# A two-layer transformer kernel: the DMA queue of SyncE put into one fixed, written order

## The chip, the cores and the metric

One core of a Trainium2 chip runs the kernel. The metric is the device time of one execution in microseconds (us), as a median over runs. All runs in this document were of the undisturbed ("fast") state. The engines are called PE (TensorE, the matrix engine), PEld (its weight loads), DVE (VectorE), ACT (ScalarE), POOL (GpSimd) and SP (SyncE, which here does nothing but issue DMA transfers). The program fixes an order for the instructions of each engine, and for the transfers that SyncE issues; the timelines below show what that does when a transfer has to wait (at the first place looked at, SyncE issues nothing for 30 us).

## The reference

`x` is 2048 tokens by 1024 channels in bfloat16. Two layers, with the same weights, each add an attention over 8 positions (its own and 7 earlier ones, every second one) and a gated feed-forward part:

```python
x = x + A(layernorm(x))       # q,k,v = x @ wqkv ; 32 heads of 32; window 8, dilation 2 ; o @ wo
x = x + B(layernorm(x))       # (relu(x @ W_gate) * (x @ W_up)) @ W_down,  inner width 3584
x = x + A(layernorm(x))
x = x + B(layernorm(x))
```

## The kernel before

The tokens are cut into 4 blocks of 512. Blocks 0 to 3 are the first layer, 4 to 7 the second, so that `n` runs from 0 to 7. The kernel is software-pipelined. For each `n`, TensorE does gate and up of block `n`, then Q, K (and V) of block `n+2`, then the output projection "wo" of block `n+1`, then the down projection of block `n` in two halves of the output channels. Meanwhile VectorE does the attention arithmetic of later blocks, and the second norm of block `n+1` is worked out during the down projection.

Weights stream through a ring of five slots of 1 MB ("slabs"). A slab may be asked for once TensorE has finished with the slab that used its slot:

```python
wring = ctx.enter_context(tc.tile_pool(name="wring", bufs=5))

def load_slab(src_ap, name):
    t = wring.tile([P, 8, SLAB], BF16, tag="slab", name=name)
    ...
    tail_sp[0] = nc.sync.dma_start(tv, src_ap).ins      # SyncE's queue
    return tv
```

The second norm, cut to what matters. Statistics and the scaled copy are on ScalarE, one power on 128 numbers is on GpSimd, and the transfer that transposes the whole block is issued, in SyncE's queue, right with the last tile:

```python
def apply(t):
    def f():
        nc.scalar.activation(xn, xt[:], ACT.Identity, scale=..., bias=...)     # normalised tile t
        if which == "b" and n == 0:
            nc.sync.dma_start_transpose(hold["xnT"][:, t, :, :], xn)
        elif t == TPB - 1:                                                     # TPB = 4 tiles of 128 tokens
            nc.sync.dma_start_transpose(hold["xnT"][...], hold["xn"][...])
    return f
# in the statistics of each tile:
#   nc.gpsimd.tensor_tensor(rstd, vpe, neg_half[:, 0:1], op=ALU.pow)
```

The down projection asks for its slab inside the step that uses it. There are eight steps, four slabs for each half:

```python
def f_(half, s8):
    def f():
        wsl = load_slab(wd_v[:, 8 * s8:8 * s8 + nfc, half * SLAB:(half + 1) * SLAB], ...)
        for t in range(TPB): ...   # 8 matmuls of 128x512 per tile, 32 per slab (half as many for the last slab of a half)
```

Everything is emitted from a list of `(time, function)` pairs sorted by time. A scheduler then fixes each engine's order, unless `tc.issue_after(ins)` pins an instruction behind another.

## Time and profile before

| | |
|---|---|
| time, median of 4 runs | 1721.78 us (1721.57 to 1723.26) |
| TensorE busy | 1637.0 us, 95% of the span of 1719.2 us |
| idle before the second half of the down projection | 56.2 us in six waits |

From the page of the kernel before, part 1 (busy us, share of the span, instructions), part 2 (40 equal slices of the span; PEclk is the granted TensorE clock in tenths, 9 standing for 90% and more) and part 4 (the chain of work that ended last):

```profile
PE 1637.0 (95%) x7576; PEld 781.2 (45%) x7576; DVE 1047.8 (61%) x888; ACT 534.5 (31%) x1117; POOL 273.7 (16%) x220
PEclk9999999899998999989999899998999989999999
PE 65%; DVE 11%; ACT 5%; POOL 4%; issue 3%; DMA 2%; SPq 2%; DVEq 0%; ACTq 0%; POOLq 0%
```

TensorE is the limit, yet the chain is on TensorE for only 65% of the span; six single slices show a lower clock. The waits of TensorE in the kernel before (engine, tile and line, what it waited for, then total us, times, longest us):

```profile
PE dacc_2642 L104 <- DMA wd_1_0_2646<-in_B_W_down_dram: 12.2, 1, 12.2
PE dacc_3999 L104 <- DMA wd_1_0_4003<-in_B_W_down_dram: 12.2, 1, 12.2
PE tp L226 <- DVE xn_first L208: 9.2, 1, 9.2
PE dacc_9780 L104 <- DMA wd_1_0_9784<-in_B_W_down_dram: 8.1, 1, 8.1
PE dacc_5446 L104 <- DMA wd_1_0_5450<-in_B_W_down_dram: 8.0, 1, 8.0
...
PE acc_g L104 <- DMA xnT_b_1207<-xn_b_1206: 5.1, 1, 5.1
PE acc_wo L104 <- DMA oT_1055<-o_d: 2.4, 1, 2.4
```

All six long waits are for `wd_1_0`, the first slab of the second half of the down projection. To see why it is late, look at SyncE's timeline at the first of them (start us, duration us, queue, line, kind of transfer, out<-in). The duration is how long SyncE took to issue the transfer, not how long it took to land (the slab at 331.87 us: 0.52 us to issue, 5.6 us from there to landing):

```profile
294.23 0.37 SPq L151 DMA_DIRECT2D wd_0_3_2613<-in_B_W_down_dram  x1
294.64 1.86 SPq L399 DMA_DIRECT2D vhm_2567<-v_d  x1
326.87 4.90 SPq L186 DMA_TRANSPOSE xnT_b_2429<-xn_b_2428  x1
331.87 0.52 SPq L151 DMA_DIRECT2D wd_1_0_2646<-in_B_W_down_dram  x1
```

SyncE issues nothing for 30 us, then the transpose, then the slab, whose slot had been free since about 301 us. TensorE's timeline (in brackets: how long it was idle before, and until what) shows the price:

```profile
324.25 1.03 PE L104 MATMUL dacc_2482<-wd_0_3_2613,hT_1392 128*128 128x512 bf16 x4
337.51 3.60 PE L104 MATMUL dacc_2642<-wd_1_0_2646,hT_1392 128*128 128x512 bf16 x8 [12.23 <-DMA wd_1_0_2646<-in_B_W_down_dram]
340.89 2.03 PE L104 MATMUL dacc_2643<-wd_1_0_2646,hT_1392 128*128 128x512 bf16 x8
```

After 12.23 us of nothing the first eight matmuls take 3.60 us where others take 1.89.

### The profile page before, as it was taken

The page shows a single profiled execution, that of the slowest core. Times are in us where ns is not written, and L with a number is a line of the kernel's source. Part 1 is how long each engine was busy: PE and PEld are TensorE (multiplying, and loading weights), DVE is VectorE, ACT ScalarE, POOL GpSimd, SP SyncE. Part 2 cuts the span into 40 slices and gives each one's busy share as a digit, 9 for nine tenths or more (in the row PEclk, how much of TensorE's full clock was granted, in tenths as well). Part 3 has the DMA queues.
Part 4 walks back from the last instruction along what each step waited for, and adds up shares of the span by engine and source line. Part 5 has one row for each costly group of instructions (what it writes and reads, how often), then busy time and mean ns, then how long its engine had stood idle before and what let it go on. Part 6 is the DMA issues. An engine that isn't in the chain of part 4 may idle for free.

```text
span 1719.2 us, 18662 instructions
## 1 busy us (share of the span) xinstructions
PE 1637.0 (95%) x7576; PEld 781.2 (45%) x7576; DVE 1047.8 (61%) x888; ACT 534.5 (31%) x1117; POOL 273.7 (16%) x220
## 2 busy tenths in 40 slices
PE   7998999799997999989999899998999989999999
PEld 3543445344553445434454344543445434444444
DVE  1699698947296854938459384692936929221211
ACT  7936412314231422314224051240513401130110
POOL 1322005301061101101042010520105100000000
PEclk9999999899998999989999899998999989999999
DMA  9476748466556483774846738458484484656442
GB/s 291 80 209 156 200 147 224 103 190 185 182 131 187 150 220 117 185 190 147 221 142 159 212 125 248 148 126 244 135 252 148 110 256 150 196 171 195 148 143 79
DMA packets 370791, 296.82 MB, mean 173 GB/s; under 512 B 142352, under 2 KB 351248, under 8 KB 369680
## 3 DMA queue, kind: packets, MB, share of 16 engines
q1 hardware_dynamic: 370416, 295.10, 60.3%
q8 instruction: 59, 0.97, 0.2%
q10 hardware_dynamic: 288, 0.52, 0.1%
q14 instruction: 28, 0.23, 0.0%
HBM read 256.77 MB, written 21.00 MB: 162 GB/s over the span
## 4 chain that ended last, share of the span: by engine, by line
PE 65%; DVE 11%; ACT 5%; POOL 4%; issue 3%; DMA 2%; SPq 2%; DVEq 0%; ACTq 0%; POOLq 0%
PE acc_g L104 23%; PE acc_u L104 22%; PE acc_q L104 3%; SPq L186 2%; PE acc_k L104 1%; POOL st_b_3784 L173 1%; PE acc_wo L104 1%; DVE ac_0_7810 L363 1%; DVE ac_0_9257 L363 1%; DVE ac_0_6367 L363 1%; POOL st_b_5235 L173 0%; POOL st_b_6679 L173 0%; POOL st_b_8122 L173 0%; PE dacc_5446 L104 0%; PE dacc_6890 L104 0%
## 5 line engine op out<-in xcount | busy, mean ns | idle before, releaser
L482 ACT ACTIVATE r<-acc_g 128x512 bf16<-128x512 f32 x224 | 132.5, 594 | 769.3 <-PE acc_g L104 760.8
L483 DVE TENSOR_TENSOR hT_10981<-acc_u,r 128x512 bf16<-128x512 f32 x28 | 19.4, 692 | 77.4 <-PE acc_u L104 77.4
L483 DVE TENSOR_TENSOR hT_9913<-acc_u,r 128x512 bf16<-128x512 f32 x28 | 19.3, 688 | 38.4 <-PE acc_u L104 38.4
L483 DVE TENSOR_TENSOR hT_8466<-acc_u,r 128x512 bf16<-128x512 f32 x28 | 19.2, 688 | 38.3 <-PE acc_u L104 36.0
L483 DVE TENSOR_TENSOR hT_4132<-acc_u,r 128x512 bf16<-128x512 f32 x28 | 19.2, 688 | 38.3 <-PE acc_u L104 36.0
L483 DVE TENSOR_TENSOR hT_2775<-acc_u,r 128x512 bf16<-128x512 f32 x28 | 19.2, 688 | 38.3 <-PE acc_u L104 36.0
L483 DVE TENSOR_TENSOR hT_7019<-acc_u,r 128x512 bf16<-128x512 f32 x28 | 19.2, 688 | 38.3 <-PE acc_u L104 36.0
L483 DVE TENSOR_TENSOR hT_5575<-acc_u,r 128x512 bf16<-128x512 f32 x28 | 19.2, 688 | 38.0 <-PE acc_u L104 35.7
L104 PEld LDWEIGHTS <-hT_1392 128*128 128x128 bf16 x224 | 22.3, 100 | 40.2 <-DMA wd_1_0_2646<-in_B_W_down_dram 12.7
L104 PEld LDWEIGHTS <-hT_2775 128*128 128x128 bf16 x224 | 22.3, 100 | 40.2 <-DMA wd_1_0_4003<-in_B_W_down_dram 12.7
L104 PEld LDWEIGHTS <-hT_8466 128*128 128x128 bf16 x224 | 22.4, 101 | 36.7 <-DMA wd_1_0_9784<-in_B_W_down_dram 8.6
L104 PEld LDWEIGHTS <-hT_7019 128*128 128x128 bf16 x224 | 22.5, 101 | 36.4 <-DMA wd_1_0_8337<-in_B_W_down_dram 8.3
L104 PEld LDWEIGHTS <-hT_5575 128*128 128x128 bf16 x224 | 22.5, 101 | 36.3 <-DMA wd_1_0_6894<-in_B_W_down_dram 8.3
L104 PEld LDWEIGHTS <-hT_4132 128*128 128x128 bf16 x224 | 22.4, 100 | 36.3 <-DMA wd_1_0_5450<-in_B_W_down_dram 8.5
L104 PEld LDWEIGHTS <-hT_9913 128*128 128x128 bf16 x224 | 21.9, 98 | 26.4
L104 PEld LDWEIGHTS <-hT_10981 128*128 128x128 bf16 x224 | 21.9, 98 | 26.4
L483 DVE TENSOR_TENSOR hT_1392<-acc_u,r 128x512 bf16<-128x512 f32 x28 | 19.2, 686 | 17.1 <-PE acc_u L104 12.6
L173 POOL TENSOR_TENSOR st_b_10661<-st_b_10661,neg_half 128x1 f32<-128x1 f32 x4 | 2.2, 550 | 159.2 <-ACT st_b_10661 L172 159.2
L329 DVE TENSOR_TENSOR prod_426<-q_0_373,k_0_411 128x4096 bf16<-128x4096 bf16 x1 | 2.3, 2293 | 27.7 <-ACT k_0_411 L296 27.7
L173 POOL TENSOR_TENSOR st_a_8704<-st_a_8704,neg_half 128x1 f32<-128x1 f32 x4 | 6.7, 1680 | 73.3 <-ACT st_a_8704 L172 73.3
L173 POOL TENSOR_TENSOR st_a_5814<-st_a_5814,neg_half 128x1 f32<-128x1 f32 x4 | 6.7, 1682 | 73.2 <-ACT st_a_5814 L172 73.2
L173 POOL TENSOR_TENSOR st_a_7257<-st_a_7257,neg_half 128x1 f32<-128x1 f32 x4 | 6.7, 1680 | 73.2 <-ACT st_a_7257 L172 73.2
(1942 smaller groups left out, 4063.1 us busy)
## 6 DMA issues: line engine op xcount, KB each, us to landing
vhm_375<-v_d SPq DMA_DIRECT2D x4, 284.0 KB, 5.4
vhm_1441<-v_d SPq DMA_DIRECT2D x4, 284.0 KB, 10.0
vhm_2567<-v_d SPq DMA_DIRECT2D x4, 284.0 KB, 9.1
vhm_3924<-v_d SPq DMA_DIRECT2D x4, 284.0 KB, 9.5
vhm_5376<-v_d SPq DMA_DIRECT2D x4, 284.0 KB, 5.8
vhm_6820<-v_d SPq DMA_DIRECT2D x4, 284.0 KB, 5.8
vhm_8263<-v_d SPq DMA_DIRECT2D x4, 284.0 KB, 5.8
vhm_9710<-v_d SPq DMA_DIRECT2D x4, 284.0 KB, 6.3
```

Source lines behind the costliest of these rows:

```text
L104: tail_pe[0] = nc.tensor.matmul(*args, **kwargs).ins
L173: nc.gpsimd.tensor_tensor(rstd, vpe, neg_half[:, 0:1], op=ALU.pow)
L186: nc.sync.dma_start_transpose(hold["xnT"][:].rearrange("p t k n -> p (t k) n"), hold["xn"][:].rearrange("p t d -> p (t d)"))
L329: nc.vector.tensor_tensor(prods[c][:], i0, i1, op=ALU.mult)
L363: nc.vector.tensor_tensor(o, ac[:], t[:], op=ALU.add)
L482: nc.scalar.activation(r[:], acc[:], ACT.Relu)
L483: nc.vector.tensor_tensor(hold["hT"][:, j, :], accs["u"][:], r[:], op=ALU.mult)
```

## The change

The intent: SyncE's order is written down in full instead of being left to the scheduler. A weight slab is asked for at the time its ring slot is planned to be free, and every other transfer gets a written place between slabs, where its data are planned to be ready. Each transfer is pinned behind the one before it. The same matmuls are done in the same order. The diff, cut to its core:

```diff
+    def sp_dma(dst, src, transpose=False):
+        start = nc.sync.dma_start_transpose if transpose else nc.sync.dma_start
+        ...
+            with tc.issue_after(tail_sp[0]):
+                tail_sp[0] = start(dst, src).ins
-    def load_slab(src_ap, name): ...
+    def want(key, src, use_end):
+        slab_plan.append((key, src, use_end))          # every slab of the kernel, with the end of its use
+    def slab_events(events):
+        for i, (key, src, _) in enumerate(slab_plan):
+            def f(...): ... sp_dma(tv, src) ...
+            events.append((slab_plan[i - RING][2] + 0.3 if i >= RING else 0.1 * i, f))
         def apply(t):
-                elif t == TPB - 1:
-                    nc.sync.dma_start_transpose(hold["xnT"]..., hold["xn"]...)
+        def turn(t=None):                               # the transpose, now an event of its own
+                    sp_dma(hold["xnT"]..., hold["xn"]..., True)
...
-            ln2(n + 1, [at + GRP * TPB + GRP * (t + 1) + 0.1 for t in range(TPB)])
+            ln2(n + 1, [at + GRP * TPB + GRP * (t + 1) + 0.1 for t in range(TPB)], at + 2 * GRP * TPB + 31.0)
...                                                      # the opening (blocks 0 to 3 before the first gate/up):
-    ln1(3, 85.0, True)
+    ln1(3, 85.0, t_v2 + 2.0, True)                      # transpose of block 3's first norm
+    ev.append((t_v2 + 3.0, store_v(1)))
+    ev.append((t_v2 + 10.0, store_o(0)))                # attention output of block 0: store, then load transposed
+    ev.append((t_v2 + 10.1, load_o(0)))
```

With the `+ 31.0` the transpose stands behind all the slabs of the down projection. Stores and loads of V and of the attention output are made events of their own in the same way.

More of the change, by code (lines that the diff above doesn't have):

```diff
@@ L56 @@
     NSL = (FC + 7) // 8
+    NSG = (FC + 3) // 4
+    RING = 5
     scale = float(DH) ** -0.5
@@ L71 @@
     dram = ctx.enter_context(tc.tile_pool(name="dram", bufs=1, space=bass.MemoryType.DRAM))
-    wring = ctx.enter_context(tc.tile_pool(name="wring", bufs=5))
+    wring = ctx.enter_context(tc.tile_pool(name="wring", bufs=RING))
     xnT_pool = ctx.enter_context(tc.tile_pool(name="xnT", bufs=2))
@@ L93 @@
     tail_sp = [None]
+    def sp_dma(dst, src, transpose=False):
+        start = nc.sync.dma_start_transpose if transpose else nc.sync.dma_start
+        if tail_sp[0] is None:
+            tail_sp[0] = start(dst, src).ins
+        else:
+            with tc.issue_after(tail_sp[0]):
+                tail_sp[0] = start(dst, src).ins
     @contextmanager
@@ L138, with load_x @@
         x_tiles.append(xt)
-    def load_x(b, alternate=False):
+    def load_x(b):
         for t in range(b * TPB, (b + 1) * TPB):
-            eng = nc.scalar if alternate and t % 2 else nc.sync
-            eng.dma_start(x_tiles[t][:], x_dram[t * P:(t + 1) * P, :])
-    load_x(0, alternate=True)
-    def load_slab(src_ap, name):
-        shp = list(src_ap.shape)
-        t = wring.tile([P, 8, SLAB], BF16, tag="slab", name=name)
-        tv = t[:, 0:shp[1], 0:shp[2]]
-        tail_sp[0] = nc.sync.dma_start(tv, src_ap).ins
-        return tv
+            if b == 0 and t % 2:
+                nc.scalar.dma_start(x_tiles[t][:], x_dram[t * P:(t + 1) * P, :])
+            else:
+                sp_dma(x_tiles[t][:], x_dram[t * P:(t + 1) * P, :])
@@ new lines, with want_v, want_qk @@
+    load_x(0)
+    slab = {}
+    slab_plan = []
+    def want(key, src, use_end):
+        slab_plan.append((key, src, use_end))
+    def want_v(key, mid, end):
+        for g in range(2):
+            want((key, g), wqkv_v[:, :, 2 * D + g * SLAB:2 * D + (g + 1) * SLAB], mid if g == 0 else end)
+    def want_qk(key, end):
+        for i, nm in enumerate(("q", "k")):
+            for hh in range(2):
+                want((key, nm, hh), wqkv_v[:, hh * (KC // 2):(hh + 1) * (KC // 2), i * D:(i + 1) * D], end)
@@ new lines, in want_wo, with want_gu, want_down @@
+    def want_wo(n, mid, end):
+        for half in range(2):
+            want(("o", n, half), wo_v[:, :, half * SLAB:(half + 1) * SLAB], mid if half == 0 else end)
+    def want_gu(n, at, gap):
+        for s in range(NSG):
+            cols = slice(s * SLAB, min((s + 1) * SLAB, F))
+            end = at + gap * min(4 * (s + 1), FC)
+            want(("g", n, s), wg_v[:, :, cols], end)
+            want(("u", n, s), wu_v[:, :, cols], end)
+    def want_down(n, at, gap):
+        for half in range(2):
+            for s in range(NSL):
+                rows = slice(8 * s, min(8 * (s + 1), FC))
+                end = at + gap * (half * FC + min(8 * (s + 1), FC))
+                want(("d", n, half, s), wd_v[:, rows, half * SLAB:(half + 1) * SLAB], end)
@@ new lines, in slab_events, with f @@
+    def slab_events(events):
+        for i, (key, src, _) in enumerate(slab_plan):
+            def f(key=key, src=src):
+                shp = list(src.shape)
+                t = wring.tile([P, 8 * SLAB], BF16, tag="slab", name="w_" + "_".join(str(k) for k in key))
+                tv = t[:, 0:shp[1] * shp[2]].rearrange("p (a b) -> p a b", b=shp[2])
+                sp_dma(tv, src)
+                slab[key] = tv
+            events.append((slab_plan[i - RING][2] + 0.3 if i >= RING else 0.1 * i, f))
@@ L179, in f @@
             def f():
-                xt = x_tiles[b * TPB + t]
-                xn = hold["xn"][:, t, :]
-                nc.scalar.activation(xn, xt[:], ACT.Identity, scale=hold["st"][:, t, 4:5], bias=hold["st"][:, t, 6:7])
-                if which == "b" and n == 0:
-                    nc.sync.dma_start_transpose(hold["xnT"][:, t, :, :], xn)
-                elif t == TPB - 1:
-                    nc.sync.dma_start_transpose(hold["xnT"][:].rearrange("p t k n -> p (t k) n"),
-                                                hold["xn"][:].rearrange("p t d -> p (t d)"))
-            return f
-        return [stats(t) for t in range(TPB)], [apply(t) for t in range(TPB)], hold
+                nc.scalar.activation(hold["xn"][:, t, :], x_tiles[b * TPB + t][:], ACT.Identity,
+                                     scale=hold["st"][:, t, 4:5], bias=hold["st"][:, t, 6:7])
+            return f
+        def turn(t=None):
+            def f():
+                if t is not None:
+                    sp_dma(hold["xnT"][:, t, :, :], hold["xn"][:, t, :], True)
+                else:
+                    sp_dma(hold["xnT"][:].rearrange("p t k n -> p (t k) n"),
+                           hold["xn"][:].rearrange("p t d -> p (t d)"), True)
+            return f
+        return [stats(t) for t in range(TPB)], [apply(t) for t in range(TPB)], turn, hold
     def ln_first():
@@ L234, with v_steps @@
     att = [{} for _ in range(NN)]
-    def v_steps(n, ln, sl=None, early=False):
-        b = n % NB
+    def v_steps(n, ln, key, early=False):
         st = att[n]
-        sl = {} if sl is None else sl
         def f_(c):
@@ L243, in f @@
                 g = c // 4
-                if g not in sl:
-                    sl[g] = load_slab(wqkv_v[:, :, 2 * D + g * SLAB:2 * D + (g + 1) * SLAB], f"wv_{n}_{g}")
                 if c == 0:
@@ L251, in f, with store_v @@
                     for kc in range(KC):
-                        mm(acc[:], lhsT=sl[g][:, kc, col:col + P], rhs=ln["xnT"][:, :, kc, :],
-                                         start=(kc == 0), stop=(kc == KC - 1))
+                        mm(acc[:], lhsT=slab[(key, g)][:, kc, col:col + P], rhs=ln["xnT"][:, :, kc, :],
+                           start=(kc == 0), stop=(kc == KC - 1))
                 nc.scalar.copy(st["vT"][:, c, :], acc[:])
-                if c == KC - 1:
-                    dst = bass.AP(tensor=v_d.tensor, offset=v_d.offset + HALO + b * BLK,
-                                  ap=[[NTOK, P], [P * NTOK, KC], [1, BLK]])
-                    nc.sync.dma_start(dst, st["vT"][:])
             return f
         return [f_(c) for c in range(KC)]
+    def store_v(n):
+        def f():
+            dst = bass.AP(tensor=v_d.tensor, offset=v_d.offset + HALO + (n % NB) * BLK,
+                          ap=[[NTOK, P], [P * NTOK, KC], [1, BLK]])
+            sp_dma(dst, att[n]["vT"][:])
+        return f
     khalo = {}
@@ L269, with qk_steps @@
     K_STEP = [QK_ORDER.index(("k", c)) for c in range(KC)]
-    def qk_steps(n, ln, sl=None):
+    def qk_steps(n, ln, key):
         b = n % NB
         st = att[n]
-        sl = {} if sl is None else sl
         def f_(nm, c):
@@ L278, in f @@
                 if nm == "q" and c == 0:
-                    for i, w in enumerate(() if sl else ("q", "k")):
-                        for hh in range(2):
-                            t = wring.tile([P, KC // 2, D], BF16, tag="slab", name=f"w{w}_{n}_{hh}")
-                            tail_sp[0] = nc.sync.dma_start(t[:], wqkv_v[:, hh * (KC // 2):(hh + 1) * (KC // 2), i * D:(i + 1) * D]).ins
-                            sl[(w, hh)] = t
                     khalo[n] = qk_pool.tile([P, KC, HALO], BF16, tag="kh", name=f"kh_{n}", bufs=2)
@@ L287, in f @@
                     for kc in range(KC):
-                        w = sl[(nm, kc // (KC // 2))][:, kc % (KC // 2), bass.ds(c, P, KC)]
+                        w = slab[(key, nm, kc // (KC // 2))][:, kc % (KC // 2), bass.ds(c, P, KC)]
                         mm(acc[:], lhsT=w, rhs=ln["xnT"][:, :, kc, :], start=(kc == 0), stop=(kc == KC - 1))
@@ L397, in f @@
                               ap=[[DH * NTOK, H], [NTOK, DH], [1, HALO + P]])
-                with tc.issue_after(tail_sp[0]):
-                    nc.sync.dma_start(att[n]["v_hm"][32 * tq:32 * tq + 32, :, :], src)
+                sp_dma(att[n]["v_hm"][32 * tq:32 * tq + 32, :, :], src)
             return f
@@ L419, in f, with store_o, load_o @@
                 nc.vector.tensor_tensor(ohm[:, g * DG:(g + 1) * DG, :], tt[:, 0], tt[:, 1], op=ALU.add)
-                if g == NG - 1:
-                    dst = bass.AP(tensor=o_d.tensor, offset=o_d[b * TPB:b * TPB + 1].offset, ap=[[DH * P, P], [1, DH * P]])
-                    nc.sync.dma_start(dst, ohm[:].rearrange("p d t -> p (d t)"))
-                    oTa = big_tile([P, KC, TPB, P], f"oT_{n}")
-                    for tq in range(TPB):
-                        src = bass.AP(tensor=o_d.tensor, offset=o_d[b * TPB + tq:b * TPB + tq + 1].offset,
-                                      ap=[[P, P], [P * P, KC], [1, P]])
-                        nc.sync.dma_start(oTa[:, :, tq, :], src)
-                    st["oT"] = oTa
             return f
         return [f_(g) for g in range(NG)]
+    def store_o(n):
+        def f():
+            b = n % NB
+            dst = bass.AP(tensor=o_d.tensor, offset=o_d[b * TPB:b * TPB + 1].offset, ap=[[DH * P, P], [1, DH * P]])
+            sp_dma(dst, att[n]["o_hm"][:].rearrange("p d t -> p (d t)"))
+        return f
+    def load_o(n):
+        def f():
+            b = n % NB
+            oTa = big_tile([P, KC, TPB, P], f"oT_{n}")
+            for tq in range(TPB):
+                src = bass.AP(tensor=o_d.tensor, offset=o_d[b * TPB + tq:b * TPB + tq + 1].offset,
+                              ap=[[P, P], [P * P, KC], [1, P]])
+                sp_dma(oTa[:, :, tq, :], src)
+            att[n]["oT"] = oTa
+        return f
     def wo_steps(n):
@@ L435, in wo_steps @@
         st = att[n]
-        sl = {}
         order = [(t, half) for t in range(TPB) for half in range(2)]
@@ L444, in f @@
                 for t, half in order[2 * i:2 * i + 2]:
-                    if half not in sl:
-                        sl[half] = load_slab(wo_v[:, :, half * SLAB:(half + 1) * SLAB], f"wo_{n}_{half}")
                     xt = x_tiles[b * TPB + t]
@@ L450, in f @@
                         for c in range(KC):
-                            mm(acc[:], lhsT=st["oT"][:, c, t, :], rhs=sl[half][:, c, :],
-                                             start=(c == 0), stop=(c == KC - 1))
+                            mm(acc[:], lhsT=st["oT"][:, c, t, :], rhs=slab[("o", n, half)][:, c, :],
+                               start=(c == 0), stop=(c == KC - 1))
                     xs = xt[:, half * SLAB:(half + 1) * SLAB]
@@ L467, in f @@
                 s4, jl = j // 4, j % 4
-                if jl == 0:
-                    ncol = min(SLAB, F - s4 * SLAB)
-                    hold["g"] = load_slab(wg_v[:, :, s4 * SLAB:s4 * SLAB + ncol], f"wg_{n}_{s4}")
-                    hold["u"] = load_slab(wu_v[:, :, s4 * SLAB:s4 * SLAB + ncol], f"wu_{n}_{s4}")
                 accs = {}
@@ L476, in f @@
                         for kc in range(KC):
-                            mm(acc[:], lhsT=hold[nm][:, kc, jl * P:(jl + 1) * P], rhs=ln["xnT"][:, :, kc, :],
-                                             start=(kc == 0), stop=(kc == KC - 1))
+                            mm(acc[:], lhsT=slab[(nm, n, s4)][:, kc, jl * P:(jl + 1) * P], rhs=ln["xnT"][:, :, kc, :],
+                               start=(kc == 0), stop=(kc == KC - 1))
                     accs[nm] = acc
@@ L498, in f @@
                 nfc = min(8, FC - 8 * s8)
-                wsl = load_slab(wd_v[:, 8 * s8:8 * s8 + nfc, half * SLAB:(half + 1) * SLAB], f"wd_{n}_{half}_{s8}")
+                wsl = slab[("d", n, half, s8)]
                 for t in range(TPB):
@@ L510, in f, with store_x @@
                         nc.vector.tensor_tensor(xs, ac[t], xs, op=ALU.add)
-                        if n >= NN - NB and half == 1:
-                            nc.sync.dma_start(out_dram[(b * TPB + t) * P:(b * TPB + t + 1) * P, :], xt[:])
             return f
         return [f_(half, s8) for half in range(2) for s8 in range(NSL)]
+    def store_x(n):
+        def f():
+            for t in range((n % NB) * TPB, (n % NB + 1) * TPB):
+                sp_dma(out_dram[t * P:(t + 1) * P, :], x_tiles[t][:])
+        return f
     def emit(events):
@@ L524, with spread @@
     GRP = 1.73
-    def spread(events, steps, at, gap):
+    def spread(steps, at, gap):
         for i, f in enumerate(steps):
-            events.append((at + gap * i, f))
+            ev.append((at + gap * i, f))
     ev = []
@@ L536, in zero_v, with ln1, ln2 @@
     def zero_v():
-        nc.sync.dma_start(bass.AP(tensor=v_d.tensor, offset=v_d.offset, ap=[[NTOK, P], [P * NTOK, KC], [1, HALO]]), zpad[:])
-    def ln1(n, at, early=False, gap=3.0):
-        stats, apply, hold = ln_steps(n, "a", early)
+        sp_dma(bass.AP(tensor=v_d.tensor, offset=v_d.offset, ap=[[NTOK, P], [P * NTOK, KC], [1, HALO]]), zpad[:])
+    def ln1(n, at, turn_at, early=False, gap=3.0):
+        stats, apply, turn, hold = ln_steps(n, "a", early)
         ln_a[n] = hold
-        spread(ev, stats, at, gap)
-        spread(ev, apply, at + 2.0 * gap, gap)
-    def ln2(n, ats):
-        stats, apply, hold = ln_steps(n, "b")
+        spread(stats, at, gap)
+        spread(apply, at + 2.0 * gap, gap)
+        ev.append((turn_at, turn()))
+    def ln2(n, ats, turn_at=None):
+        stats, apply, turn, hold = ln_steps(n, "b")
         ln_b[n] = hold
@@ L550, in ln2 @@
             ev.append((a + 4.0, apply[t]))
-    wqk, wv23 = {}, {}
-    ev.append((12.0, zero_v))
-    ev.append((13.0, lambda: load_x(1)))
-    spread(ev, v_steps(0, ln_a[0], early=True), 15.0, GRP)
-    ln1(1, 20.0, True)
-    at = 29.0
-    gap = 2.1
-    spread(ev, qk_steps(0, ln_a[0], wqk), at, gap)
+            if turn_at is None:
+                ev.append((a + 9.0, turn(t)))
+        if turn_at is not None:
+            ev.append((turn_at, turn()))
+    GAP0 = 2.05
+    t_v0 = 15.0
+    t_qk0 = t_v0 + GRP * KC
@@ new lines @@
+    t_qk1 = t_qk0 + GAP0 * 2 * KC
+    t_v1 = t_qk1 + GRP * 2 * KC + 1.5
+    t_v2 = t_v1 + GRP * KC
+    t_wo0 = t_v2 + GRP * KC
+    t_v3 = t_wo0 + GRP * KC
+    t_gu0 = t_v3 + GRP * KC
+    ev.append((0.45, zero_v))
+    ev.append((0.5, lambda: load_x(1)))
+    want_v("v0", t_v0 + GRP * KC / 2, t_qk0)
+    want_qk("qk01", t_v1)
+    spread(v_steps(0, ln_a[0], "v0", early=True), t_v0, GRP)
+    ln1(1, 22.0, 47.5, True, 5.0)
+    ev.append((t_qk0 + 1.5, store_v(0)))
+    spread(qk_steps(0, ln_a[0], "qk01"), t_qk0, GAP0)
@@ L561 @@
     mults, reds = prod_direct_steps(0)
     for c in range(KC):
-        ev.append((at + gap * (K_STEP[c] + 1.0), mults[c]))
+        ev.append((t_qk0 + GAP0 * (K_STEP[c] + 1.0), mults[c]))
         if c < KC - 2:
-            ev.append((at + gap * (K_STEP[c] + 2.5), reds[c]))
-    spread(ev, load_v_steps(0), 31.0, 7.0)
-    ev.append((45.0, lambda: load_x(2)))
-    at += gap * 2 * KC
-    spread(ev, qk_steps(1, ln_a[1], wqk), at, GRP)
-    ev.append((at + 0.5 * GRP, reds[KC - 2]))
-    ev.append((at + 1.5 * GRP, reds[KC - 1]))
@@ L572 @@
-    ev.append((at + 1.6 * GRP, lambda: softmax(0)))
-    spread(ev, pv_steps(0), at + 10.0, 4.2)
-    ln1(2, 60.0, True)
-    ev.append((70.0, lambda: load_x(3)))
-    sums1, red1 = prod_sum_steps(1)
-    spread(ev, sums1, at + 46.0, 4.4)
-    at += GRP * 2 * KC
-    spread(ev, v_steps(1, ln_a[1], wv23, True), at, GRP)
-    at += GRP * KC
-    ln1(3, 85.0, True)
-    spread(ev, v_steps(2, ln_a[2], wv23, True), at, GRP)
-    at += GRP * KC
-    spread(ev, wo_steps(0), at, 2 * GRP)
-    ln2(0, [at + 2 * GRP * (t + 1) + 0.1 for t in range(TPB)])
@@ L586 @@
-    at += 2 * GRP * TPB
-    spread(ev, v_steps(3, ln_a[3], wv23), at, GRP)
-    at += GRP * KC
-    spread(ev, load_v_steps(1), at + 6.0, 9.0)
-    ev.append((at + 48.1, red1))
-    ev.append((at + 48.2, lambda: softmax(1)))
-    ev.append((at - 0.01, start_hidden))
+            ev.append((t_qk0 + GAP0 * (K_STEP[c] + 2.5), reds[c]))
+    spread(load_v_steps(0), t_qk0 + 5.0, 6.0)
+    ev.append((50.0, lambda: load_x(2)))
+    spread(qk_steps(1, ln_a[1], "qk01"), t_qk1, GRP)
+    ev.append((t_qk1 + 0.5 * GRP, reds[KC - 2]))
@@ new lines @@
+    ev.append((t_qk1 + 1.5 * GRP, reds[KC - 1]))
+    ev.append((t_qk1 + 1.6 * GRP, lambda: softmax(0)))
+    spread(pv_steps(0), t_qk1 + 10.0, 4.2)
+    ln1(2, 60.0, t_qk1 + 15.0, True)
+    ev.append((70.0, lambda: load_x(3)))
+    want_v("v123", t_v3 + GRP * KC / 2, t_gu0)
+    spread(v_steps(1, ln_a[1], "v123", True), t_v1, GRP)
+    ln1(3, 85.0, t_v2 + 2.0, True)
+    ev.append((t_v2 + 3.0, store_v(1)))
+    spread(v_steps(2, ln_a[2], "v123", True), t_v2, GRP)
+    ev.append((t_v2 + 10.0, store_o(0)))
@@ new lines @@
+    ev.append((t_v2 + 10.1, load_o(0)))
+    ev.append((t_wo0 + 3.0, store_v(2)))
+    sums1, red1 = prod_sum_steps(1)
+    spread(sums1, t_qk1 + 46.0, 4.4)
+    want_wo(0, t_v3, t_v3)
+    spread(wo_steps(0), t_wo0, 2 * GRP)
+    ln2(0, [t_wo0 + 2 * GRP * (t + 1) + 0.1 for t in range(TPB)])
+    spread(v_steps(3, ln_a[3], "v123"), t_v3, GRP)
+    ev.append((t_gu0 + 3.0, store_v(3)))
+    spread(load_v_steps(1), t_gu0 + 6.0, 7.0)
+    ev.append((t_gu0 + 48.1, red1))
+    ev.append((t_gu0 + 48.2, lambda: softmax(1)))
@@ L594 @@
+    ev.append((t_gu0 - 0.01, start_hidden))
+    at = t_gu0
     for n in range(NN):
         gu, hold = gu_steps(n, ln_b[n])
-        spread(ev, gu, at, 2 * GRP)
+        want_gu(n, at, 2 * GRP)
+        spread(gu, at, 2 * GRP)
         if n == 0:
-            spread(ev, pv_steps(1), at + 58.0, 5.5)
+            spread(pv_steps(1), at + 58.0, 5.5)
+            ev.append((at + 105.0, store_o(1)))
+            ev.append((at + 105.1, load_o(1)))
         elif n + 1 < NN:
@@ L601 @@
             ev.append((at + 0.2, lambda n=n: softmax(n + 1)))
-            spread(ev, pv_steps(n + 1), at + 12.0, 6.5)
+            spread(pv_steps(n + 1), at + 12.0, 6.5)
+            ev.append((at + 72.0, store_o(n + 1)))
+            ev.append((at + 72.1, load_o(n + 1)))
         if n + 2 < NN:
-            ln1(n + 2, at + 30.0)
+            ln1(n + 2, at + 30.0, at + 58.0)
         at += 2 * GRP * FC
         if n + 2 < NN:
-            spread(ev, qk_steps(n + 2, ln_a[n + 2]), at, GRP)
-            sums, red = prod_sum_steps(n + 2)
-            reds_n[n + 2] = red
-            spread(ev, sums, at + GRP * (K_STEP[0] + 1.0), 4.4)
+            want_qk(("qk", n + 2), at + 2 * GRP * KC)
+            spread(qk_steps(n + 2, ln_a[n + 2], ("qk", n + 2)), at, GRP)
+            sums, reds_n[n + 2] = prod_sum_steps(n + 2)
+            spread(sums, at + GRP * (K_STEP[0] + 1.0), 4.4)
             at += 2 * GRP * KC
             if n + 2 >= NB:
-                spread(ev, v_steps(n + 2, ln_a[n + 2]), at, GRP)
+                want_v(("v", n + 2), at + GRP * KC / 2, at + GRP * KC)
+                spread(v_steps(n + 2, ln_a[n + 2], ("v", n + 2)), at, GRP)
                 at += GRP * KC
+                ev.append((at + 3.0, store_v(n + 2)))
         if n + 1 < NN:
-            spread(ev, wo_steps(n + 1), at, 2 * GRP)
-            ln2(n + 1, [at + GRP * TPB + GRP * (t + 1) + 0.1 for t in range(TPB)])
+            want_wo(n + 1, at + GRP * TPB, at + 2 * GRP * TPB)
+            spread(wo_steps(n + 1), at, 2 * GRP)
+            ln2(n + 1, [at + GRP * TPB + GRP * (t + 1) + 0.1 for t in range(TPB)], at + 2 * GRP * TPB + 31.0)
             at += 2 * GRP * TPB
         if n + 2 < NN:
-            spread(ev, load_v_steps(n + 2), at + 8.0, 9.0)
-        down = down_steps(n, hold)
-        spread(ev, down, at, 4 * GRP)
+            spread(load_v_steps(n + 2), at + 4.0, 6.5)
+        want_down(n, at, GRP / 2)
+        spread(down_steps(n, hold), at, 4 * GRP)
         at += GRP * FC
+        if n >= NN - NB:
+            ev.append((at + 4.0, store_x(n)))
+    slab_events(ev)
     emit(ev)
```

## The prediction

> **What bounds it now.** TensorE: 1637.0 of 1719.2 us busy (page, part 1), at granted clock 0.978. The list of waits gives TensorE about 78 us of idle time. 56.2 us of it is six waits of one kind: the first matmul of the second half of the down projection waits 12.2, 12.2, 8.1, 8.0, 7.9 and 7.8 us for its weight slab. The rest: 9.2 before the first transpose, 5.1 for the first transposed second-norm activations, 2.4 for the attention output, and small ones.
>
> **Why the slab is late.** In SyncE's timeline nothing is issued from 296.5 to 326.87 us: the transpose of the second norm's activations stands there, waiting for ScalarE's last normalised tile. It then takes 4.90 us to issue, and the slab behind it, whose ring slot had been free since about 301 us, is asked for at 331.87 and lands about 5.6 us later. TensorE finished the first half at 325.1 and restarts at 337.5. [...] one waiting transfer held all behind it.
>
> After each gap the first eight matmuls take 3.60 us instead of 1.89. [...] (granted clock 0.82 in that stretch). By gate/up starts the periods are 201.3, 211.3, 211.4, 211.5, 211.7 us; counting matmuls at 0.216 us gives (my estimate) 187.1 without a V stage and 201.0 with one. So a stall costs 14.2 us twice and about 10.4 four times: 70 us, all on TensorE's path.
>
> **What the change does.** No compute is added or removed; matmul order is the same. I compared, in the built programs, the matmul after which each transfer may go with the one that first needs it. The transpose moves behind the down slabs; every second-half slab then has 113 matmuls (24 us) of lead, against 5 to 8 us landings. The transpose itself keeps 24 us[...]. The shortest lead, 37 matmuls (8 us, last K slab), is as before; that slab lands in 5.3. VectorE frees the PSUM banks in time (744.4 us where the third tile would start at 745.0). So I expect all six stalls gone: minus 70.
>
> **The opening may lose a little.** Weights now go ahead of the second block's x; ScalarE's statistics for block 2 move behind the last K copy (about 64 us), so its copies of K1 and Q4 of block 1 come late and TensorE, with six PSUM banks, may wait 2 to 6 us near 88 us; perhaps 2 more near 48 us. The 2.4 us attention wait (plus 1.7 of slow clock) should be absorbed.  Net estimate plus 3.
>
> **Prediction: 1655 us, 1645 to 1670.** Faster by over 2%: 0.95; within 2%: 0.04; slower: 0.01.
>
> **Right or wrong would show:** no waits on second-half down slabs; gate/up periods near 187 and 201 us; no 30 us silence on SyncE at the transpose; TensorE's clock near 1.0 in down stages; first gate/up matmul at 158 to 166 us (160.7 before). Wrong if a period stays above 205 (a transfer still stands in the way, or PSUM release or the transpose now ends last), or the opening grows by over 10 us.

Three clauses are cut from the text, at the marks. None is a term of its sum: 1721.8 us, less 70 for the six stalls, plus 3 for the opening, is the 1655 us. For the transfers that it counts on, the kernel before shows this: issuing the transpose of a block took 4.8 to 6.7 us, and it had landed 6.7 to 8.8 us after its issue began; the full weight slabs landed in 5.0 to 13.1 us, 116 of 159 of them in 8.0 or less.

## The result, and the profile after

The kernel after takes 1652.39 us (median of 4 runs, 1651.39 to 1653.87), against 1721.78 before. The ratio is 0.9596, with a 95% interval of 0.9579 to 0.9613. A ratio here is always the mean time of one kernel's fast runs over that of the other's fast runs in the same rounds, so it is not quite the ratio of the medians quoted.

The page of the kernel after, the lines that answer to those above:

```profile
PE 1623.2 (98%) x7576; PEld 778.2 (47%) x7576; DVE 1048.1 (64%) x888; ACT 534.6 (32%) x1117; POOL 276.3 (17%) x220
PEclk9998999999999999999999999999999999999999
PE 90%; issue 0%; DVE 0%; ACT 0%; DMA 0%
```

TensorE's own busy time is 13.8 us smaller although it does the same 7576 matmuls: mostly because they no longer run at the slow clock after each long wait (six times 3.60 us for eight matmuls that otherwise take 1.89, my estimate about 10 us; the mean granted clock rose from 0.978 to 0.997). The waits of TensorE after:

```profile
PE tp L279 <- DVE xn_first L261: 9.0, 1, 9.0
PE acc_wo L115 <- DMA oT<-o_d: 6.5, 1, 6.5
PE acc_g L115 <- issue: 2.4, 1, 2.4
PE acc_v L115 <- ACT vT L303: 1.7, 1, 1.7
```

No wait on a down slab is left. One wait has grown: that for the attention output `oT`, from 2.4 to 6.5 us. SyncE's timeline after, in the same stage as above:

```profile
303.00 0.59 SPq L104 DMA_DIRECT2D vhm<-v_d  x1
309.49 0.37 SPq L104 DMA_DIRECT2D w_d<-in_B_W_down_dram  x1
309.92 0.76 SPq L104 DMA_DIRECT2D vhm<-v_d  x1
316.40 0.37 SPq L104 DMA_DIRECT2D w_d<-in_B_W_down_dram  x1
...
326.76 0.37 SPq L104 DMA_DIRECT2D w_g<-in_B_W_gate_dram  x1
328.31 6.41 SPq L104 DMA_TRANSPOSE xnT_b<-xn_b  x1
```

The slabs now go out as slots come free, every 6.9 us, which is 32 matmuls. The transpose goes at 328.31 instead of 326.87: it is no earlier, it only no longer holds anything that TensorE needs soon. TensorE's timeline has all 224 matmuls of the down projection in one piece:

```profile
302.39 48.51 PE L115 MATMUL dacc<-w_d,hT 128*128 128x512 bf16 x224
```

Where did the time go? The first gate/up matmul starts at 161.96 us instead of 160.71, so the opening lost 1.25 us. From there to the end it is 1488.2 us instead of 1558.5 (spans 1650.2 and 1719.2 less these starts), so the loop gained 70.3 us. The prediction had a loss of 3 and a gain of 70. The gain is firm, the loss is not: when the kernel after was profiled a second time (run `after_again`, experiment 6), the loop took 1488.3 us again, but the first gate/up matmul started at 164.01 us, a loss of 3.3. The difference lies in the last wait of the opening, 2.4 us here and 4.6 us there, which the profile puts down to "issue". In both runs TensorE goes on 3.2 us after the transpose of block 0's last second-norm tile was issued (158.74 and 160.83 us), as in the kernel before (157.51), so I read it as the wait for that tile.

### The profile page after: what moved, and what is told of

It reads as the page before. It is cut to its first block, busy times and chain, and to the rows that moved or that the text cites. A ratio compares the mean times of both kernels' runs of the same rounds, so it can differ in the third digit from the quotient of the medians.

```text
span 1650.2 us, 18654 instructions
## 1 busy us (share of the span) xinstructions
PE 1623.2 (98%) x7576; PEld 778.2 (47%) x7576; DVE 1048.1 (64%) x888; ACT 534.6 (32%) x1117; POOL 276.3 (17%) x220
## 4 chain that ended last, share of the span: by engine, by line
PE 90%; issue 0%; DVE 0%; ACT 0%; DMA 0%
PE acc_g L115 24%; PE dacc L115 23%; PE acc_u L115 23%; PE acc_wo L115 6%; PE acc_k L115 5%; PE acc_q L115 5%; PE acc_v L115 3%; PE L L115 0%; DVE x L556 0%; ACT vT L303 0%; DMA xnT_b<-xn_b 0%
## 5 line engine op out<-in xcount | busy, mean ns | idle before, releaser
L115 PE MATMUL acc_g<-xnT_b,w_g 128*128 128x512 bf16 x1792 | 425.0, 380 | 2.4 <-issue 2.4
L115 PE MATMUL acc_u<-xnT_b,w_u 128*128 128x512 bf16 x1792 | 423.3, 379 | 0.0
L115 PE MATMUL dacc<-w_d,hT 128*128 128x512 bf16 x1792 | 388.1, 379 | 0.0
L529 DVE TENSOR_TENSOR hT<-acc_u,r 128x512 bf16<-128x512 f32 x224 | 153.5, 687 | 322.0 <-PE acc_u L115 308.3
L115 PEld LDWEIGHTS <-w_g 128*128 128x128 bf16 x1792 | 175.0, 98 | 216.4 <-issue 7.5
L115 PEld LDWEIGHTS <-w_u 128*128 128x128 bf16 x1792 | 175.4, 98 | 211.8 <-issue 0.6
L115 PEld LDWEIGHTS <-hT 128*128 128x128 bf16 x1792 | 175.3, 98 | 211.4
L399 DVE TENSOR_TENSOR t<-q,k 128x2048 f32<-128x2048 bf16 x98 | 223.6, 2289 | 9.8 <-ACT k L342 6.6
L409 DVE TENSOR_TENSOR ac<-ac,t 128x2048 f32<-128x2048 f32 x84 | 191.8, 2283 | 0.4
L461 DVE TENSOR_TENSOR pv<-a,vhm 128x4096 bf16<-128x4096 bf16 x64 | 145.2, 2282 | 0.0
```

Of the source, the lines that this page charges most:

```text
L115: tail_pe[0] = nc.tensor.matmul(*args, **kwargs).ins
L399: nc.vector.tensor_tensor(t[:], i0, i1, op=ALU.mult)
L409: nc.vector.tensor_tensor(o, ac[:], t[:], op=ALU.add)
L461: nc.vector.tensor_tensor(tt[:], a_bc, v_sh, op=ALU.mult)
L529: nc.vector.tensor_tensor(hold["hT"][:, j, :], accs["u"][:], r[:], op=ALU.mult)
```

## The experiments

The first theory (T1) is that of the prediction: one waiting transfer at the head of SyncE's queue holds a slab that could go. The rival (T2) is that the fixed order as a whole does it: slabs asked for by slot, other transfers spread out, less contention. Every kernel of this section gave the correct result. "Ratio" is against the kernel before in the same rounds.

### 1. Only the one transfer moved

The kernel before, with the transpose of blocks 1 to 7 emitted after the step that asks for the third slab of the second half:

```diff
-                elif t == TPB - 1:
+                elif which == "a" and t == TPB - 1:
...
+        def turn():
+            with tc.issue_after(tail_sp[0]):
+                tail_sp[0] = nc.sync.dma_start_transpose(...).ins
...
         spread(ev, down, at, 4 * GRP)
+        if n + 1 < NN:
+            ev.append((at + 28.0 * GRP - 4 * GRP + 0.1, ln_b[n + 1]["turn"]))
```

> The kernel before, with one thing changed: the transposes of the second norm's activations of blocks 1 to 7 stand behind the third slab of the second half of the down projection instead of ahead of its first slab. Weights are still asked for in the step that uses them, and the opening is untouched. Theory T1 (one waiting transfer at the head of SyncE's queue held a slab whose slot was free): all six waits of 7.8 to 12.2 us on the second-half down slab vanish, gate/up periods near 187 and 201 us, opening as before, 1650 to 1655 us. Rival T2 (the gain comes from the fixed order as a whole: weights asked for by slot, the spacing of the other transfers, less contention): moving this one kind of transfer gives little, 1700 us or more.

Measured: 1651.07 us (1650.96 to 1651.34), ratio 0.9586 [0.9572, 0.9601]. SyncE's timeline of this run (x2 stands for two transfers in one line, from the start of the first to the end of the second):

```profile
301.68 7.28 SPq L151 DMA_DIRECT2D wd<-in_B_W_down_dram  x2
309.00 0.76 SPq L405 DMA_DIRECT2D vhm<-v_d  x1
315.49 0.37 SPq L151 DMA_DIRECT2D wd<-in_B_W_down_dram  x1
327.41 4.87 SPq L192 DMA_TRANSPOSE xnT_b<-xn_b  x1
332.38 0.53 SPq L151 DMA_DIRECT2D wd<-in_B_W_down_dram  x1
```

No wait on a down slab is left. One transfer moved gives the whole gain; T2 is out as the main cause. The transpose still waits until 327 us, and one slab still stands behind it, but that one is the last of the half and has time.

### 2. Only the one transfer put back

The kernel after, with the transpose ahead of the first slab of the second half again:

```diff
-            want_wo(n + 1, at + GRP * TPB, at + 2 * GRP * TPB)
-            ln2(n + 1, [...], at + 2 * GRP * TPB + 31.0)
+            want_wo(n + 1, at + GRP * TPB, at + 2 * GRP * TPB + 4.0)   # so that the slab's event comes after it
+            ln2(n + 1, [...], at + 2 * GRP * TPB + 4.2)
```

> The kernel after, with one thing put back: the transpose of the second norm's activations stands in SyncE's written order directly ahead of the first slab of the second half of the down projection, as in the kernel before. All else of the fixed order stays. T1: the six waits of about 12, 12, 8, 8, 8, 8 us come back, with the slow-clock stretch after each: about 1722 us (1652 plus 70; 1715 to 1728). T2: below 1670 us, since the fixed order as a whole is kept.

Measured: 1723.44 us (1722.50 to 1724.23), ratio 1.0008 [0.9991, 1.0025]. Its waits of TensorE begin with:

```profile
PE dacc L115 <- DMA w_d<-in_B_W_down_dram: 57.1, 6, 12.4
```

All six waits are back, 57.1 us against 56.2 before. SyncE is again silent, for 31.7 us, before the transpose at 328.06 us, and the slab follows it at 332.86. The interval also says what the rest of the change is worth: with this one transfer put back, the fixed order of all the others is within 0.25% of the kernel before.

### 3. The dose between

The kernel after, with the transpose between the first and the second slab of the second half (`+ 31.0` became `+ 6.0`).

> The dose between the two: the kernel after with the transpose one slab later than in the previous run, between the first and the second slab of the second half of the down projection. T1: the slab behind the transpose is now the second, which TensorE needs 32 matmuls (6.9 us) later, so each wait shrinks by 6.9 us: from 12.2 to about 5.3 us twice, from about 8 to about 1 us four times; with about 2 us of slow clock after the two long ones, 15 to 22 us over the kernel after: 1667 to 1674 us. T2: no more than 5 us over the kernel after.

Measured: 1678.93 us (1674.93 to 1682.44), ratio 0.9747 [0.9729, 0.9766]. That is 26.5 us over the kernel after, and more than expected. Its waits of TensorE:

```profile
PE dacc L115 <- DMA w_d<-in_B_W_down_dram: 19.1, 6, 7.5
...
PE acc_g L115 <- issue: 4.6, 1, 4.6
```

The direction and the form fit T1: the waits of the profiled run are 7.5 and 6.0 us in the first two stages and 1.3 to 1.6 us in the other four. The size was missed for two reasons that the trace shows. In the first stage the slab behind the transpose was asked for at 335.68 us and landed 7.7 us later (TensorE goes on at 343.40), not 5.6 as I had assumed; other transfers that had queued up went out with it, which is my reading of the reason, though no run tests it (in the kernel before, the three slabs that went out one after another behind the transpose, from 331.87 us on, landed in 5.6, 8.4 and 11.3 us). And the opening happened to be 2.3 us longer (first down matmul at 304.68 against 302.39 us), with a 4.6 us wait for `acc_g`, as in the second profile of the unchanged kernel after.

### 4. The waiting transfer in another queue

The kernel before, with the same transposes issued from ScalarE's queue and nothing else changed:

```diff
-                    nc.sync.dma_start_transpose(...)
+                    (nc.scalar if which == "b" else nc.sync).dma_start_transpose(...)
```

> The kernel before with the transposes of the second norm's activations of blocks 1 to 7 issued from ScalarE's queue, where their source is made, instead of SyncE's; SyncE's order is otherwise unchanged. T1 (the transfer that waits must not stand in the queue that feeds TensorE): the six long waits vanish, 1650 to 1660 us; the transpose is issued as soon as its last tile is there, and its about 5 us of issue now lie on ScalarE, which has little to do in the down stage. Rival T2 (the fixed order as a whole is the gain, as against the order of before): 1700 us or more. A third outcome, waits of 3 to 6 us in the down stage, would say that a transpose under way slows or stops other transfers, whichever queue it is in.

Measured: 1650.92 us (1650.10 to 1651.81), ratio 0.9584 [0.9571, 0.9597]. ScalarE's timeline shows the transpose right behind the tile that it waited for:

```profile
325.41 1.24 ACT L182 ACTIVATE xn_b<-x,st_b 128x1024 bf16<-128x1024 bf16 x1
326.68 6.34 ACTq L186 DMA_TRANSPOSE xnT_b<-xn_b  x1
```

It is issued at the same time as before, but from where its waiting hurts nobody, and the six waits are gone. Meanwhile SyncE goes on asking for slabs (300.94 us and after). So it was the queue position, not the transpose's own work, that cost the time.

### 5. Why is the transposed tile late at all?

The transpose waits for ScalarE, and ScalarE for GpSimd's power on 128 numbers. From GpSimd's timeline of the kernel before, one of these powers in the opening and two in the first down stage:

```profile
33.46 0.55 POOL L173 TENSOR_TENSOR st_a_265<-st_a_265,neg_half 128x1 f32<-128x1 f32 x1 [3.62 <-ACT st_a_265 L172]
...
301.97 2.01 POOL L173 TENSOR_TENSOR st_b_2427<-st_b_2427,neg_half 128x1 f32<-128x1 f32 x1 [10.74 <-ACT st_b_2427 L172]
309.19 7.00 POOL L173 TENSOR_TENSOR st_b_2427<-st_b_2427,neg_half 128x1 f32<-128x1 f32 x1 [5.21 <-ACT st_b_2427 L172]
```

The same instruction takes 0.55 us or 7.00 us. In the second place VectorE is running products and sums of 128x2048 with two inputs and float32 results, 2.3 us each, back to back. My theory of the lateness (T3) was that these VectorE instructions hold GpSimd's up. To test it, the kernel before was run with SyncE's, TensorE's and ScalarE's orders unchanged, but VectorE's second half of the partial sums (in the second layer's blocks only the last quarter) held until the last of these powers was done:

```diff
+                def gate(n=n):            # a 128x1 copy on VectorE that waits for the last power
+                    with tc.issue_after(last_add[0]):
+                        gate_ins[0] = nc.vector.tensor_copy(g[:], ln_b[n + 1]["st"][:, TPB - 1, 4:5]).ins
...
-            spread(ev, sums, at + GRP * (K_STEP[0] + 1.0), 4.4)
+            spread(ev, sums[:k], at + GRP * (K_STEP[0] + 1.0), 4.4)
+                spread(ev, [held(f) for f in sums[k:]], at + 0.3, 4.4)    # issued after the gate
```

> What makes the transposed tiles so late? In the kernel before, GpSimd's power on 128 numbers takes 0.55 us in the quiet opening but 2.0 to 7.0 us in this stage, while VectorE runs two-input operations of 2.3 us back to back; ScalarE waits for it. This is the kernel before with SyncE's, TensorE's and ScalarE's orders unchanged: only VectorE's second half of the partial sums is held, by a one-column copy that waits for the last of these powers, until the norm's statistics are done. T3 (the lateness comes from GpSimd held up by VectorE): the powers take about 0.6 us, the transpose is issued about 10 us earlier in the first two stages (about 316 instead of 326.9 us), the slab behind it is asked for in time, waits shrink to 0 to 2 us each: 1650 to 1662 us although the transfer still stands in the same place. Rival: ScalarE's own work or the additions on VectorE make it late; then the powers may be short but the waits stay above 6 us, 1695 us or more. Held sums could also end too late for the next softmax; that would show as a wait before the L matmuls.

Measured: 1686.39 us (1686.18 to 1686.86), ratio 0.9790 [0.9776, 0.9803]: half of the gain. GpSimd's timeline and then SyncE's, each in the first down stage:

```profile
310.70 0.55 POOL L175 TENSOR_TENSOR st_b<-st_b,neg_half 128x1 f32<-128x1 f32 x1 [5.21 <-ACT st_b L174]
313.52 0.55 POOL L175 TENSOR_TENSOR st_b<-st_b,neg_half 128x1 f32<-128x1 f32 x1 [2.27 <-ACT st_b L174]
```

```profile
318.70 4.92 SPq L188 DMA_TRANSPOSE xnT_b<-xn_b  x1
323.72 1.20 SPq L153 DMA_DIRECT2D wd<-in_B_W_down_dram  x2
```

The last three of the stage's four powers, with the sums held, take 0.55 us each (the first, before that, still 2.01), so the slowness did come from what VectorE was running (T3's first half). The transpose is issued at 318.70 us, 8.2 us earlier, or 9.7 us earlier counted from the stage's first down matmul (302.45 against 300.94 us). The waits on the slab fall from 56.2 to 21.2 us, the longest being 4.1 us. They do not vanish, so my expectation of 1650 to 1662 us failed. The rest, in this stage, is ScalarE's own chain of statistics and copies for four tiles, which ends at 318.7 us almost without the hold-up, and the 4.9 us that the transpose takes to issue. As long as the transfer stands in front of the slab, making it ready earlier helps only in part.

### 6. Three tries on the opening

The wait for `oT` that grew to 6.5 us is the same mechanism in another place. SyncE's timeline of the kernel after, in the opening:

```profile
112.83 4.82 SPq L104 DMA_TRANSPOSE xnT_a<-xn_a  x1
117.74 0.53 SPq L104 DMA_DIRECT2D v_d<-vT  x1
118.37 0.58 SPq L104 DMA_DIRECT2D o_d<-ohm  x1
125.75 2.95 SPq L104 DMA_DIRECT2D oT<-o_d  x4
```

VectorE has finished `ohm`, the attention output, at 111.2 us, but its store stands behind a transpose that waits for ScalarE until 112.8 us and takes 4.8 us to issue. TensorE needs `oT` at 122.5 us. In the kernel before, the order was the same, but VectorE finished `ohm` only at 116.9 us, when the transpose had gone (108.78), so it did not show.

First try: store and loads of the attention output ahead of that transpose.

```diff
-    ln1(3, 85.0, t_v2 + 2.0, True)
+    ln1(3, 85.0, t_v2 + 10.2, True)
```

> A try to beat both, on the other place where a transfer waits behind another: in the opening of the kernel after, the store and the four loads of the first block's attention output now stand ahead of the transpose of block 3's first-norm activations instead of behind it. T1 (same mechanism as in the down stage): the store goes at about 111 us, when VectorE has finished its source, instead of at 118.4; the 6.5 us wait of TensorE on the attention output vanishes or shrinks under 1 us, with about 1.7 us of slow clock; 1643 to 1647 us. Rival: the wait is set by the store's and loads' own time or by the transfers around them, then at least 4 us of it stays and the time is within 2 us of the kernel after; or the transpose, now later, makes a new wait at block 3's V stage.

Measured: 1650.37 us (1648.07 to 1652.08), ratio 0.9581 [0.9567, 0.9596]. The waits of this run:

```profile
PE acc_g L115 <- DMA xnT_b<-xn_b: 6.1, 1, 6.1
PE acc_wo L115 <- DMA oT<-o_d: 1.8, 1, 1.8
```

The wait for `oT` fell, to 1.8 us where under 1 was expected: the store, still behind the store of V (114.46 us), went at 114.92 and not at 111. Most of the gain went into the next wait, for the second norm's last transposed tile, which grew from 2.4 to 6.1 us. The expected 1643 to 1647 us was missed, and the interval overlaps that of the kernel after. That chain (additions on VectorE between its long sums, powers on GpSimd, statistics on ScalarE) ended at 155.4 us, only 3.3 us earlier than in the kernel after (158.7).

Second try: in addition, VectorE's partial sums of block 1 held until the last addition of the output projection.

```diff
-    spread(sums1, t_qk1 + 46.0, 4.4)
+    spread(sums1[:3], t_qk1 + 46.0, 4.4)
+    spread([held(f) for f in sums1[3:]], t_v3 + 4.0, 3.4)      # issued after the last addition
```

> A second try to beat both. In the last try (attention output ahead of the transpose) TensorE's wait of 6.5 us fell to 1.8 us, but the next wait, for the last transposed tile of the second norm of block 0, grew to 6.1 us: the chain of additions on VectorE, powers on GpSimd and statistics on ScalarE ended at 155.4 us. Here VectorE's partial sums of block 1 are held in addition until the last addition of the output projection of block 0, so that additions come at once and GpSimd is not held up. Theory: the chain ends at about 147 to 150 us, the 6.1 us wait and about 1.7 us of slow clock vanish: 1641 to 1645 us. Rival: ScalarE's in-order work alone takes that long; the wait stays above 3 us and the time is over 1647 us.

> The kernel after once more, unchanged, beside the others on this chip: about 1652 us.

Measured: 1649.52 us (1647.74 to 1649.88), ratio 0.9571 [0.9558, 0.9584]; the kernel after beside it 1654.26 us, ratio 0.9599 [0.9586, 0.9612]. The expected 1641 to 1645 us was missed. The wait for the transposed tile fell to 2.2 us, but that for `oT` was 2.3 us and the L matmuls of block 1 now waited 1.9 us for the later sums.

Third try, on top of the second: block 1's store of V behind the loads of `oT`, the sums held until the last power of that norm, and the L matmuls of block 1, with what follows them, 7 us later.

```diff
-    ev.append((t_v2 + 3.0, store_v(1)))
+    ev.append((t_v2 + 10.2, store_v(1)))
+    ev.append((t_v3 + 4.0, gate))                              # as in experiment 5
-    ev.append((t_gu0 + 48.1, red1))
+    ev.append((t_gu0 + 55.1, red1))                            # and softmax, P.V, store and load of o a little later
```

> A third try on the opening, on top of the last (attention output ahead of the transpose, partial sums held). Three changes: the store of block 1's V, which stood ahead of the attention output's store and was itself waiting for ScalarE until 114.4 us while the attention output was ready at 112.4, now stands behind the loads; the partial sums are held until the last of the second norm's powers of block 0 (the last try's power at 145.5 us took 1.58 us again, once VectorE had gone on); and the L matmuls of block 1 with all that follows them stand 7 us later, as the sums now end later. If the chain is as read: the attention output's wait of 2.3 us falls under 0.5 us, the 2.2 us wait for the transposed tile vanishes, no new wait before L: 1642 to 1646 us. If ScalarE's in-order work is what ends last, the 2.2 us wait stays and the time is within 2 us of the last try's 1649.5 us.

Measured: 1646.01 us (1645.57 to 1647.34), ratio 0.9561 [0.9548, 0.9574]. It has the lowest time of all, at the upper edge of what was expected. Its interval lies clear of those of the kernel after, but overlaps that of the second try, and the two were not run in the same rounds. Its waits of TensorE, the first two:

```profile
PE tp L280 <- DVE xn_first L262: 8.8, 1, 8.8
PE acc_g L116 <- ACT r L529: 3.6, 1, 3.6
```

Both waits of the opening are gone. The store of the attention output, issued at 110.92 us, had landed when the loads went at 114.80, 3.9 us later; behind the store of V it had taken 7.4 us (118.37 to 125.75 in the kernel after). The first gate/up matmul starts at 150.66 us instead of 161.96. But 11.3 us earlier there became only 6.3 us at the end (spans 1643.9 and 1650.2): VectorE now has its deferred sums in the gate/up stage, and TensorE waits there for ScalarE (3.6 us, at 185.5 us) and once for VectorE (0.9 us), and runs slow for a stretch after the first (8 matmuls in 3.46 us). The 3.6 us wait is the same pattern once more, in ScalarE's own order: the copy `r` that TensorE waits for (184.87 us) stands behind the next norm's statistics, which had waited 2.86 us for a power on GpSimd that took 3.78 us beside VectorE's sums (the first norms' powers of this run average 1.43 us, against 0.55 us in the quiet opening of the kernel before).

## Why the prediction was right, and where it was not

- **Bound and cause: right, and shown by runs.** The six waits come from the transpose at the head of SyncE's queue. Moving it alone gives the whole gain (experiment 1), putting it back alone takes all of it away (2), half-way gives part (3), another queue cures it too (4). SyncE's silence of 30 us (296.5 to 326.87 us) shows the wait at the issuing side; experiment 4 changes the issuing engine and its DMA queue together.
- **Size of the stalls: right.** 70 us were predicted and the loop gained 70.3. The estimate held because the slow stretch after each wait was counted with the wait: 14.2 us for 12.2 us of idle, 10.4 for about 8. The predicted periods of 187.1 and 201.0 us are met: the L matmuls follow each other at 354.28, 541.42 and 742.36 us, which makes 187.1 and 200.9. The clock in the stretch from 300 to 350 us rose from 0.86 to 1.00.
- **Signs to look for: all seen.** No waits on second-half down slabs, no 30 us silence before the transpose, first gate/up at 161.96 us within the predicted 158 to 166.
- **The opening: the net about right by luck, two of its terms wrong.** Plus 3 was predicted, plus 1.25 and plus 3.3 were measured in two profiles. "TensorE, with six PSUM banks, may wait 2 to 6 us near 88 us" did not happen: its V matmuls of block 1 start at 92.88 us, 1.85 us *earlier* than before (94.73). This lead was lost at once, in a 1.65 us wait for ScalarE's copies of V at 108.5 us. And "the 2.4 us attention wait ... should be absorbed" failed: it grew to 6.5 us. I had compared the transfers in the down stage one by one with what they wait for, but not those of the opening, where the order `transpose, store of V, store of attention output` was unchanged; VectorE came 5.7 us earlier to it and found the queue held. This put TensorE 5.1 us behind the kernel before (block 3's V at 145.59 against 140.45 us). Most of it did not reach the end, because the waits that follow shrank: that for the last transposed tile from 5.1 to 2.4 us (4.6 in the second profile), and one of 1.0 us for ScalarE's copy was gone. The prediction counts on neither, so the closeness of 1655 to 1652.4 us owes something to chance.
- **What the prediction did not ask:** why ScalarE's tile comes so late. Experiment 5 shows that about half of the cost of the queue position came from GpSimd being held up by VectorE.

## What to carry to other kernels

SyncE sent its transfers in their written order here: the slab whose slot was free at about 301 us went out at 331.87, behind the transpose. Such a queue must not have, ahead of a transfer that the critical engine needs soon, one that waits for a slow producer: look for a silence in the issuing engine's timeline that ends with a transfer of another kind, and move that one transfer (behind, or to another queue) before rewriting the whole order. Here one moved transfer did what the rewrite of the whole order did. A silence alone is not enough: the kernel after still has one of 29.9 us, before the transpose at 86.56 us in the opening, and TensorE waits for nothing behind it. Then follow where the gained time goes: in the opening each cured wait handed a part of its gain to the next wait in the chain. The version that beats both kernels changed the queue order, VectorE's order and the time of a consumer together; no run tells which of these it could do without.

## What else the traces show

- TensorE ran slow after short idle gaps too: after 2.27 us of idle 64 matmuls took 15.67 us instead of 13.99 (second try), after 2.75 us 112 took 26.03 instead of 24.34 (experiment 5), about 1.7 us each. After 1.81 us nothing was lost (64 in 13.99 us, first try), but nor was it after 3.48 us (64 in 13.99 us, experiment 1), so these runs give no sharp limit.
- Every later transfer of SyncE's queue was held by the one that waited: in the kernel before, the transpose made a silence of 22 to 30 us on SyncE in each of six stages, and cost 70 us over the six.
- Issuing a transpose of 128x4096 bfloat16 held the engine for 4.7 us (experiment 2, at 328.06 us) to 9.8 us (kernel after, at 1197.22 us), against 0.4 to 0.6 us for most slabs of 1 MB, so a slab behind a transpose is late by that too (331.87 us, behind the 4.90 us from 326.87).
- A small GpSimd instruction beside VectorE's products and sums became slow: 0.55 us became 2.0 to 7.0 us on 128 numbers in the first two down stages. The 7.0 us (309.19 to 316.19; the profile's spans on GpSimd are rough, but ScalarE waits 5.9 us for this one) spans three VectorE instructions of 2.3 us, so one small instruction stood over more than one of them. What about those VectorE instructions holds GpSimd up is not shown; experiment 5 shows only that they cause it.
